# A separate queue for the weight differences of a Strassen-Winograd MLP behind lightning attention, with a new order of loads

## The chip, the cores and the metric

The kernel runs on one core of one Trainium2 chip. The metric is device time in microseconds (us), the median of three runs. Five engines matter: TensorE (PE) multiplies matrices, VectorE (DVE), ScalarE (ACT) and GpSimd (POOL) work elementwise, and the queue of SyncE (SP) starts every load and store. Each engine works off its own instruction stream in order: an instruction that waits holds up all that stands behind it on that engine.

## The reference

```python
# q, k, v: (4, 8, 768, 64), lam: (8,), w_in: (512, 2048), w_out: (2048, 512), all float32; block = 64
for b in range(nb):
    intra = np.einsum('bhic,bhjc->bhij', qb, kb) * Dmask[None]
    intra = np.einsum('bhij,bhjd->bhid', intra, vb)
    inter = np.einsum('bhid,bhde->bhie', qb * lam_pow[None], kv_state)
    out[:, :, sl] = intra + inter
    kv_state = lam_block * kv_state + np.einsum('bhsd,bhse->bhde', kb * rev_pow[None], vb)
x = out.transpose(0, 2, 1, 3).reshape(3072, 512)
h = x @ w_in
g = np.maximum(0.01 * h, h)
return g @ w_out
```

Lightning attention runs in blocks of 64 tokens, with a state per head that is carried from block to block. Its result, 3,072 tokens of 512 values, goes through a two-layer MLP with a leaky ReLU. The weights reach the chip as 64-bit numbers (512 KB for 128 x 512 of them), and the kernel turns them into float32 itself.

## The kernel before

**Attention.** The tokens come in 24 chunks of 128 (six for each batch element). `load` (L328) fetches one chunk: k and q in two pieces each, v in one, 768 KB in all. A chunk passes through a step of three parts (`step`, L481): the products and sums of the chunk before (`own`, `inter`), the transposes of k and q (`transpose_k`, `transpose_q`), and the scores with the update of the state (`scores`, `kv`, `sums_kv`). The copies of the transposes are on ACT, the masking of the scores (`sc`, L403), the update of the state (L430) and, at first, the scaling of q (`qsT`, L388) on DVE, the decay of k (L379) and of the state (L433) on POOL.

**The MLP.** Four chunks make a group (six groups, g), and the hidden dimension is cut into four units (u). For each (g, u) there is an `up` (L568) and a `down` (L600). Each is one step of Strassen-Winograd: seven products P1 to P7 of half-size blocks instead of eight, each of eight 128 x 128 x 256 matmuls. There are 48 stages of `up` or `down` (6 x 4 x 2), so 336 products. The products come in the order P1, P2, P6, P5, P7, P3, P4. P1 and P2 need only blocks of the weights as they are; P6, P5 and P4 need the *differences* of weight blocks T2, T1 and T4 (L318), and P6, P5, P7 and P3 need sums of the left operand (`xs` for `up`, `gS` for `down`, L555). Two PSUM banks, Z and W, alternate; a product waits until the bank was copied or added off (`keep` on ACT or DVE, `total` on DVE).

**The weights.** They come in 32 blocks of 128 hidden columns (n = 0 to 31): for unit u, four blocks of w_in (wi), then four of w_out (wo). Blocks n and n+1 (n even) make a pair, pair n // 2. `load_w` (L217) fetches a block, `conversion` (L244) queues what makes float32 of it: on ACT `magnitude`, `low_part`, `sign_part` (L270, L281, L284); for a pair on DVE `clamp`, `shift`, `first`, `low` (L289, L293, L298 twice); then three subtractions T1, T2, T4 (L305), on DVE for the pairs in `T_DVE`, on POOL for the others.

**The order of the work.** The instruction streams are written by a planner that runs when the kernel is built. It keeps a clock for each engine (`clk`) and an estimated time at which each result is ready. `run` (L176) emits one piece of work. Before that it fills the wait: the conversions lie in the lists `later["ACT"]`, `later["DVE"]`, `later["POOL"]`, first in, first out, and `emit` takes the head of the engine's list when by the estimate it ends no later than the awaited input plus `SLACK`. The slack is 0.55 us while `alone` is true, that is, while attention runs with no MLP beside it, and zero after that. `need(n)` (L199) emits everything that belongs to blocks below n, whatever the clocks say, and then issues every load that has room. `pump` (L209) issues loads in the order of the string `LOADS` ("c" a chunk, "w" a weight block), passing over those that have no room yet (a chunk c needs chunk c-3 finished), as long as the clock of the loads is less than `AHEAD` in front of the PE's.

The kernel begins with nine parts (three steps) of attention alone, then `need(4)`, the rest of what chunk 2 and the front of what chunk 3 needs, P1 and P2 of the first `up` with the scores and state of chunk 3 between, `early(3)`, the sums of the first group (`x_sums(0)`), and `FIRST` parts of the next step (L668 to L679). After that, each `up` or `down` takes along as many parts of attention as `STEPS` says for it (L680 to L684):

```python
    for n, (g, u, w) in enumerate((g, u, w) for g in range(NG) for u in range(NU) for w in range(2)):
        need((2 * u + w + 1) * NW // (2 * NU))
        together((up, down)[w](g, u) if n else parts, STEPS[n] if n < len(STEPS) else 3 * (w == 0))
```

Of the kernel before, what the change touches and what calls it, by code (L numbers as in the profile page):

```python
# [59 lines left out]
def kernel(  # L60
# [20 lines left out]
    NCH = B * NCB  # L81
    GC = 4
    NG = NCH // GC
    T = GC * C // 2
# [72 lines left out]
    ROOMS = ["st"] + [f"{w}{p}" for w, p, h in reversed(blocks) if h == 0 and p >= UP]  # L157


    LOADS = "cwwcwwcwccwwwcwwwccccwcwwwwwwwwwwwwwwwwwwww" + "c" * NCH  # L160
    SLACK, AHEAD = (0.55, 0), (8.0, 14.0)

    T_DVE = [0, 1, 3, 7, 9, 11, 14]

    FIRST, STEPS = 2, [3, 2, 1, 5, 4, 6, 3, 4, 0, 0, 1, 2, 0, 0, 0, 4]
    rooms = {}
    w_raw, lo, w_done = {}, {}, 0

# [2 lines left out]


    clk = {"PE": 0.0, "ACT": 2.0, "DVE": 8.0, "POOL": 1.0, "DMA": 0.5}
    ready, later = {}, {"ACT": [], "DVE": [], "POOL": []}

    def run(eng, us, fn, after=(), gives=None, fill=True):  # L176
        t = max([ready.get(k, 0.0) for k in after], default=0.0)
        if fill and eng in later:
            while later[eng] and emit(eng, t + SLACK[alone]):
                pass  # L180
        clk[eng] = max(clk[eng], t) + us
        fn()
        if gives is not None:
            ready[gives] = clk[eng] + 0.1
        if eng != "DMA":
            pump()

    def emit(eng, until):

        can, us, fn, after, gives = later[eng][0]  # L190
        if not can() or any(k not in ready for k in after):
            return False
        if max([clk[eng]] + [ready[k] for k in after]) + us > until:
            return False
        later[eng].pop(0)
        run(eng, us, fn, after, gives, fill=False)
        return True

    def need(n):  # L199

        while any(later[e] and later[e][0][4][1] < n for e in later):
            m = sum(map(len, [*later.values(), *loads.values()]))
            for e in later:
                while later[e] and later[e][0][4][1] < n and emit(e, 1e9):
                    pass
            pump(urgent=True)
            assert sum(map(len, [*later.values(), *loads.values()])) < m

    def pump(urgent=False):  # L209
        while urgent or clk["DMA"] < clk["PE"] + AHEAD[fin > 3]:  # L210
            able = [x for x in sorted(y[0] for y in loads.values() if y) if x[2]()]
            if not able:
                return
            loads[able[0][1]].pop(0)
            able[0][3]()

    def load_w(n):  # L217
        w, p, h = blocks[n]
        f = p + NP * h
        rooms[n] = room_free(n)  # L220
        pool, size = (tp, 2 * d_model) if rooms[n] == "st" else (wop, 7 * QB)
        t = pool.tile([P, size], F32, name="ws", tag=rooms[n], bufs=1)
        w_raw[n] = t[:, 0:2 * d_model].bitcast(I64)

        def go():
            if w == "wi":
                nc.sync.dma_start(out=w_raw[n].rearrange("p (ko f) -> p ko f", ko=KO), in_=w_in_r[:, :, f * P:(f + 1) * P])
            else:
                nc.sync.dma_start(out=w_raw[n], in_=moe_w_out[f * P:(f + 1) * P, :])

        run("DMA", 1.95, go, [("lowp", m) for m in range(n) if rooms[m] == rooms[n]], ("raw", n))
        ready["raw", n] += 2.0
# [5 lines left out]
    def taken():  # L238
        return {rooms[m] for m in w_raw}
# [4 lines left out]
    def conversion(n, first):  # L244

        kind, p, h = blocks[n]
        W, s = (WI, SI) if kind == "wi" else (WO, SO)

        def dest():
            return W[p][:, 0:4:3, :] if (kind == "wi") == (h == 0) else W[p][:, 1:3, :]

        def words(i, dt):
            return w_raw[n].bitcast(dt).rearrange("p (n two) -> p n two", two=2)[:, :, i].rearrange("p (a b) -> p a b", a=2)

        def may():
            return h == 1 or n <= w_done + 2 and f"{kind}{p}" not in taken()

        def magnitude():
            if h == 0:
                W[p] = wop.tile([P, 7, QB], F32, name=f"{kind}{p}", tag=f"{kind}{p}")
            nc.scalar.activation(out=dest(), in_=words(1, F32), func=AF.Abs)  # L270

        def addend(dt, i):
            t = lo[n].rearrange("p (a b) -> p a b", a=2).bitcast(dt)
            return t.rearrange("p a (b two) -> p a b two", two=2)[:, :, :, i]

        def low_part():
            if h == 0:
                lo[n] = W[p][:, 4:6, :].rearrange("p a b -> p (a b)").bitcast(I32)
            else:
                lo[n] = tp.tile([P, d_model], I32, name="lo", tag="lo", bufs=1)  # L280
            nc.scalar.activation(out=addend(U16, 0), in_=words(0, U32), func=AF.Copy, bias=0.0, scale=2.0 ** -29)  # L281

        def sign_part():
            nc.scalar.activation(out=addend(BF16, 1), in_=words(1, F32), func=AF.Sign, bias=tiny[:, 0:1])  # L284
            del w_raw[n]

        def clamp():
            d = W[p][:, 0:4, :].rearrange("p a b -> p (a b)")
            nc.vector.tensor_scalar(d, d, HI_MIN, HI_MAX, op0=ALU.max, op1=ALU.min)  # L289

        def shift():
            d = W[p][:, 0:4, :].rearrange("p a b -> p (a b)").bitcast(I32)
            nc.vector.tensor_scalar(d, d, 3, None, op0=ALU.logical_shift_left)  # L293

        def low():
            nonlocal w_done
            d = dest().bitcast(I32)
            nc.vector.tensor_tensor(d, d, lo.pop(n).rearrange("p (a b) -> p a b", a=2), op=ALU.add)  # L298
            w_done = n + 1

        def yes():
            return True

        def part(out, a, b, m):
            return lambda: e.tensor_tensor(*(W[p][:, s[i]:s[i] + m, :] for i in (out, a, b)), op=ALU.subtract)  # L305

        later["ACT"].append((may, 0.67, magnitude, [("raw", n)], ("mag", n)))
        later["ACT"].append((lambda: h == 0 or n < w_done + 2, 0.78, low_part, [("raw", n)], ("lo", n)))
        later["ACT"].append((yes, 0.87, sign_part, [("raw", n)], ("lowp", n)))
        if h == 0:  # L310
            return low
        later["DVE"].append((yes, 0.95, clamp, [("mag", n)], ("c", n - 1)))
        later["DVE"].append((yes, 0.95, shift, [], ("s", n - 1)))
        later["DVE"].append((yes, 0.84, first, [("lowp", n - 1)], ("w", n - 1)))
        later["DVE"].append((yes, 0.84, low, [("lowp", n)], ("w", n)))
        eng, e = ("DVE", nc.vector) if n // 2 in T_DVE else ("POOL", nc.gpsimd)

        for o, x, y, m in (("T1", "B12", "B11", 2), ("T2", "B22", "T1", 1), ("T4", "B21", "T2", 1)):  # L318
            us = {"DVE": 0.15 + 0.27 * m, "POOL": 0.13 + 0.75 * m}[eng]
            later[eng].append((yes, us, part(o, x, y, m), [("w", n)], (o, n)))  # L320

    loads = {"c": [], "w": []}

# [4 lines left out]
    def load(c):  # L328
        b, s0 = c // NCB, (c % NCB) * C
        t = []  # L330
        for src, nm, bufs in ((k, "k", 3), (q, "q", 2), (v, "v", 3)):
            x = ldp.tile([P, H, D], F32, name=nm, tag=nm, bufs=bufs)
            y = src[b, :, s0:s0 + C, :]

            def go():
                if nm == "v":
                    nc.sync.dma_start(out=x, in_=y.rearrange("h p d -> p h d"))
                else:
                    for i in range(2):
                        nc.sync.dma_start(out=x[:, i * HP:(i + 1) * HP, :], in_=y[i::2].rearrange("h p d -> p h d"))  # L340

            run("DMA", 1.35, go, [("fin", c - 3)], (nm, c))
            ready[nm, c] += 2.0
            t.append(x)
        loaded[c] = t
# [290 lines left out]
                       lambda name: [PROD[name][0], ("sum", "DVE", PROD[name][0])], u > 0)  # L636


    todo, alone = [], True

    def together(parts, n):

# [13 lines left out]
    for n in range(NW):  # L656
        first = conversion(n, first)
    for i, x in enumerate(LOADS):
        n = len(loads[x])
# [7 lines left out]

    together([], 3 * GC - 3)  # L668
    need(NW // (2 * NU))
    parts, (own_2, whole_3, quads_3) = up(0, 0), step()  # L670
    own_2()
    whole_3()
    alone = False
    parts.pop(0)()
    quads_3()
    parts.pop(0)()
# [38 lines left out]
```

## Time and profile before

| | |
|---|---|
| median of three runs | 701.74 us (700.93 to 703.64) |
| span of the profiled execution | 702.0 us |
| PE busy | 677.3 us (96%) |
| DVE, ACT, POOL busy | 333.4, 217.5, 144.3 us |
| matmuls of the 336 products (L584, L610) | some 0.38 us each as recorded; a product takes 1.73 us |
| subtractions T1, T2, T4 (L305) | 21 on DVE, 27 on POOL |
| loads | 24 chunks of 768 KB, 32 weight blocks of 512 KB |

The page of a profile gives the busy time of each engine, then the span in 40 slices (17.6 us each) with busy shares in tenths, the granted PE clock and the load on the DMA engines. A table of waits names, for each engine, the instruction that stood and the one that released it. The timeline lists instructions in order of time with the idle time before each in brackets, and the table by stages gives the busy time of each engine in chosen stretches. A load counts as landed here when the last of its sixteen completion records in the trace has come.

### The profile page before, as it was taken

The page shows a single profiled execution, that of the slowest core. Times are in us where ns is not written, and L with a number is a line of the kernel's source. Part 1 is how long each engine was busy: PE and PEld are TensorE (multiplying, and loading weights), DVE is VectorE, ACT ScalarE, POOL GpSimd, SP SyncE. Part 2 cuts the span into 40 slices and gives each one's busy share as a digit, 9 for nine tenths or more (in the row PEclk, how much of TensorE's full clock was granted, in tenths as well). Part 3 has the DMA queues.
Part 4 walks back from the last instruction along what each step waited for, and adds up shares of the span by engine and source line. Part 5 has one row for each costly group of instructions (what it writes and reads, how often), then busy time and mean ns, then how long its engine had stood idle before and what let it go on. Part 6 is the DMA issues. An engine that isn't in the chain of part 4 may idle for free.

```text
span 702.0 us, 13353 instructions
## 1 busy us (share of the span) xinstructions
PE 677.3 (96%) x5834; PEld 582.9 (83%) x5834; DVE 333.4 (47%) x493; ACT 217.5 (31%) x361; POOL 144.3 (21%) x139
## 2 busy tenths in 40 slices
PE   6787999999999999999999999999999999999997
PEld 4566888788888888888888888888888888888886
DVE  4769899966314325314245233352433344234324
ACT  4567866551321211321202223113122112221210
POOL 2435355846001005200105102103100003000000
PEclk8879999999999999999999999999999999999999
DMA  9997176533201003302202211000100000100001
GB/s 224 255 268 216 46 202 175 134 96 75 78 1 31 1 0 92 77 1 46 46 1 47 64 43 31 1 2 1 61 1 0 1 0 16 46 0 1 1 0 61
DMA packets 93146, 42.81 MB, mean 61 GB/s; under 512 B 76704, under 2 KB 91040, under 8 KB 93088
## 3 DMA queue, kind: packets, MB, share of 16 engines
q1 hardware_dynamic: 92944, 41.95, 22.4%
q8 instruction: 46, 0.75, 0.5%
q14 instruction: 12, 0.10, 0.1%
q10 hardware_dynamic: 144, 0.00, 0.0%
HBM read 35.66 MB, written 6.29 MB: 60 GB/s over the span
## 4 chain that ended last, share of the span: by engine, by line
PE 87%; DVE 7%; POOL 1%; ACT 1%; DMA 1%; SPq 1%; issue 1%; DVEq 0%; ACTq 0%
PE Z L584 23%; PE Z L610 21%; PE W L584 18%; PE W L610 16%; PE po L351 3%; PE pt L367 2%; PE ps L351 2%; DVE gS L555 2%; PE pu L351 1%; DVE gA L555 1%; DVE wi L298 1%; POOL xs L555 1%; DMA q<-in_q_dram 1%; DVE wi L305 1%; SPq L340 1%
## 5 line engine op out<-in xcount | busy, mean ns | idle before, releaser
L610 PE MATMUL Z<-wo,gA 128*128 128x256 f32 x576 | 137.7, 382 | 0.5 <-DVE os L528 0.5
L610 PEld LDWEIGHTS Z<-wo,gA 128*128 128x128 f32 x576 | 107.5, 190 | 15.3 <-DVE os L528 0.6
L584 PE MATMUL Z<-xs,wi 128*128 128x256 f32 x384 | 92.8, 385 | 3.0 <-DVE xs L555 3.0
L584 PE MATMUL W<-xs,wi 128*128 128x256 f32 x384 | 92.9, 385 | 0.0
L584 PE MATMUL Z<-x,wi 128*128 128x256 f32 x384 | 91.5, 381 | 0.9 <-DVE gA L534 0.9
L610 PE MATMUL W<-wo,gA 128*128 128x256 f32 x384 | 90.8, 379 | 0.0
L530 ACT COPY gA<-Z 128x512 f32<-128x512 f32 x48 | 28.1, 586 | 196.1 <-PE Z L584 196.1
L584 PEld LDWEIGHTS Z<-xs,wi 128*128 128x128 f32 x384 | 73.7, 193 | 13.5 <-DVE xs L555 3.2
L546 ACT ACTIVATE gA<-gA 128x512 f32<-128x512 f32 x72 | 45.3, 630 | 118.5 <-DVE gA L534 118.5
L584 PEld LDWEIGHTS Z<-x,wi 128*128 128x128 f32 x384 | 72.2, 190 | 10.9 <-DVE gA L534 1.1
L610 PEld LDWEIGHTS W<-wo,gA 128*128 128x128 f32 x384 | 72.8, 190 | 9.9
L584 PEld LDWEIGHTS W<-xs,wi 128*128 128x128 f32 x384 | 72.5, 192 | 10.1
L379 POOL TENSOR_TENSOR k<-k,decay 128x512 f32<-128x512 f32 (+1 forms) x24 | 28.1, 1172 | 226.8 <-PE pt L367 221.8
L534 DVE TENSOR_TENSOR gA<-gA,W 128x512 f32<-128x512 f32 x48 | 33.0, 687 | 85.6 <-PE W L584 85.6
L534 DVE TENSOR_TENSOR gA<-gA,Z 128x512 f32<-128x512 f32 x24 | 16.5, 687 | 98.8 <-PE Z L584 98.8
L610 PE MATMUL Z<-wo,gS 128*128 128x256 f32 x192 | 46.0, 382 | 2.7 <-POOL qsT L388 2.2
L610 PE MATMUL W<-wo,gS 128*128 128x256 f32 x192 | 46.1, 383 | 2.3 <-DVE os L534 2.3
L584 PE MATMUL W<-x,wi 128*128 128x256 f32 x192 | 46.4, 385 | 0.0
L534 DVE TENSOR_TENSOR os<-os,W 128x512 f32<-128x512 f32 x48 | 32.8, 683 | 22.4 <-PE W L610 22.4
L610 PEld LDWEIGHTS W<-wo,gS 128*128 128x128 f32 x192 | 35.8, 189 | 8.9 <-DVE os L534 4.1
L610 PEld LDWEIGHTS Z<-wo,gS 128*128 128x128 f32 x192 | 35.9, 190 | 8.5 <-POOL qsT L388 2.6
L433 POOL TENSOR_TENSOR state<-state,pow_q 128x256 f32<-128x256 f32 x40 | 28.4, 709 | 69.0 <-DVE state L430 62.2
(79 smaller groups left out, 741.1 us busy)
## 6 DMA issues: line engine op xcount, KB each, us to landing
ws<-in_moe_w_in_dram SPq DMA_DIRECT2D x16, 512.0 KB, 5.8
ws<-in_moe_w_out_dram SPq DMA_DIRECT2D x16, 512.0 KB, 5.3
k<-in_k_dram SPq DMA_DIRECT2D x48, 128.0 KB, 3.8
q<-in_q_dram SPq DMA_DIRECT2D x48, 128.0 KB, 3.0
v<-in_v_dram SPq DMA_DIRECT2D x24, 256.0 KB, 4.2
out_dram<-os SPq DMA_DIRECT2D x23, 256.0 KB, 2.5
out_dram<-os SPq DMA_DIRECT2D x2, 128.0 KB, 1.8
lam_b<-in_lam_dram ACTq DMA_DIRECT2D x1, 4.0 KB, 2.7
```

Source lines behind the costliest of these rows:

```text
L298: nc.vector.tensor_tensor(d, d, lo.pop(n).rearrange("p (a b) -> p a b", a=2), op=ALU.add)
L305: return lambda: e.tensor_tensor(*(W[p][:, s[i]:s[i] + m, :] for i in (out, a, b)), op=ALU.subtract)
L351: nc.tensor.matmul(out[HALF[cols]], lhsT=lhsT[HALF[rows]], rhs=rhs[HALF[rows]], start=start, stop=True, skip_group_check=True)
L367: nc.tensor.transpose(out=pt[:, y, :], in_=loaded[c][i][:, 2 * y:2 * y + 2, :].rearrange("p a d -> p (a d)"), identity=ident)
L379: run("POOL", 1.2, lambda: nc.gpsimd.tensor_tensor(kr[n], kr[n], _bc(pow_k, 3, D)[n], op=ALU.mult), [("pt", "k")], ("kd", c))
L433: run("POOL", 0.8, lambda: nc.gpsimd.tensor_tensor(state[(m + 1) % 4], new, _bc(lam_c, 2, D), op=ALU.mult), [("state", m)], ("lstate", m + 1))
L530: run("ACT", 0.6, lambda: nc.scalar.copy(dst(i), st[tag]), [tag], f"keep{i}")
L534: lambda: nc.vector.tensor_tensor(dst(i), dst(i), st[tag], op=ALU.add), [f"keep{i}", tag], f"tot{i}")
L546: run("ACT", 0.64, lambda: nc.scalar.activation(out=dst, in_=src, func=AF.Prelu, bias=0.0, scale=1.0, alpha=0.01), [after], gives)
L555: run(eng, us, lambda: e.tensor_tensor(t[o], t[a], t[b], op=op), after, ("sum", eng, o))
L584: nc.tensor.matmul(t[:, i, :], lhsT=w[:, kk, :], rhs=x[:, kk, :], start=(first and i == 0 and kk == 0), stop=(i == UP - 1 and kk == 1), sk ...
L610: nc.tensor.matmul(t[:, m, :], lhsT=G[g, u][sa][:, i, m * P:(m + 1) * P], rhs=WO[UP * u + i][:, SO[sb], :], start=(first and m == 0 and i ...
```

## The change

Three things change, none of which alters what is computed.

The differences T1, T2 and T4 leave the lists of the conversions and get lists of their own, "DVE T" and "POOL T". A list of this kind is looked at after the engine's plain list, and as long as the new flag `held` is true nothing is taken from it, by `run` or by `need`. `held` falls together with `alone`, just ahead of the first product. So while attention runs alone, DVE gets no differences in between, and later they yield to the conversions of the following blocks until `need` calls for them.

The loads come in another order: chunks 1 and 2 each come one weight block after the chunk before instead of two, so that four chunks and four blocks lead instead of four chunks and five blocks, and chunk 4 comes after weight blocks 4 to 7.

The numbers of the plan follow: `SLACK` and `AHEAD` are larger, the pairs whose differences run on DVE are others (pair 1 goes to POOL; 13 and 15 go to DVE), and the parts of attention are spread otherwise over the first sixteen stages (35 parts as before).

```diff
-    LOADS = "cwwcwwcwccwwwcwwwccccwcwwwwwwwwwwwwwwwwwwww" + "c" * NCH
-    SLACK, AHEAD = (0.55, 0), (8.0, 14.0)
-    T_DVE = [0, 1, 3, 7, 9, 11, 14]
-    FIRST, STEPS = 2, [3, 2, 1, 5, 4, 6, 3, 4, 0, 0, 1, 2, 0, 0, 0, 4]
+    LOADS = "cwcwcwwcwwwwcwwwcccwcwwcwwwwwwwwwwwwwwwwww" + "c" * NCH
+    SLACK, AHEAD = (0.7, 0), (10.0, 16.0)
+    T_DVE = [0, 3, 7, 9, 11, 13, 14, 15]
+    FIRST, STEPS = 2, [2, 2, 1, 5, 5, 6, 3, 3, 0, 0, 0, 3, 0, 1, 0, 4]
...
-    ready, later = {}, {"ACT": [], "DVE": [], "POOL": []}
+    ready, later = {}, {"ACT": [], "DVE": [], "DVE T": [], "POOL T": []}
...
-        if fill and eng in later:
-            while later[eng] and emit(eng, t + SLACK[alone]):
+        for e in (eng, eng + " T") if fill else ():
+            while later.get(e) and emit(e, t + SLACK[alone]):
                 pass
...
-        can, us, fn, after, gives = later[eng][0]
-        if not can() or any(k not in ready for k in after):
+        can, us, fn, after, gives = later[queue][0]
+        eng = queue.split()[0]
+        if not can() or held and eng != queue or any(k not in ready for k in after):
             return False
...
-        while any(later[e] and later[e][0][4][1] < n for e in later):
+        queues = [e for e in later if not (held and " " in e)]
+        while any(later[e] and later[e][0][4][1] < n for e in queues):
...
-            later[eng].append((yes, us, part(o, x, y, m), [("w", n)], (o, n)))
+            later[eng + " T"].append((yes, us, part(o, x, y, m), [("w", n)], (o, n)))
...
-    todo, alone = [], True
+    todo, alone, held = [], True, True
...
-    alone = False
+    alone = held = False
```

More of the change, by code (lines that the diff above doesn't have):

```diff
@@ L186, in run, with emit @@
             pump()
-    def emit(eng, until):
-        can, us, fn, after, gives = later[eng][0]
-        if not can() or any(k not in ready for k in after):
+    def emit(queue, until):
+        can, us, fn, after, gives = later[queue][0]
+        eng = queue.split()[0]
+        if not can() or held and eng != queue or any(k not in ready for k in after):
             return False
@@ L194, in emit @@
             return False
-        later[eng].pop(0)
+        later[queue].pop(0)
         run(eng, us, fn, after, gives, fill=False)
@@ L199, in need @@
     def need(n):
-        while any(later[e] and later[e][0][4][1] < n for e in later):
+        queues = [e for e in later if not (held and " " in e)]
+        while any(later[e] and later[e][0][4][1] < n for e in queues):
             m = sum(map(len, [*later.values(), *loads.values()]))
-            for e in later:
+            for e in queues:
                 while later[e] and later[e][0][4][1] < n and emit(e, 1e9):
```

## The prediction

> **What bounds the kernel now.** I read the page's slices first, then the PE's waits, then the timeline of the first 65 us. The slices (17.6 us each):
>
> ```profile
> PE   6787999999999999999999999999999999999997
> DVE  4769899966314325314245233352433344234324
> ...
> PEclk8879999999999999999999999999999999999999
> DMA  9997176533201003302202211000100000100001
> ```
>
> After slice 4 the PE is full to the end; before it, it has holes and a reduced clock, just where the DMA engines are at 9. The stage table says what is left to win:
>
> ```profile
> 26.40:180.00 153.60, 142.31 (x1844) 119.84 (x1843) 122.35 (x166) 90.37 (x148) 79.09 (x71) 0.97 0.59 163
> 180.00:690.00 510.00, 508.98 (x3563) 442.71 (x3562) 190.21 (x282) 111.63 (x190) 56.16 (x52) 1.00 0.08 21
> ```
>
> The columns are stage, length, PE, weight load, DVE, ACT, POOL, clock, DMA share and GB/s. From the first product (26.4) to 180 us the PE stands 153.6 - 142.3 = 11.3 us; from 180 to 690 us only 1.0 us. The products are the same 336 afterwards, so this edit can only win or lose in the first 180 us. The PE's waits:
>
> ```profile
> PE Z L584 <- DVE xs L555: 3.0, 1, 3.0
> PE po L351 <- DVE sc L403: 2.4, 3, 1.2
> PE W L610 <- DVE os L534: 2.3, 3, 1.7
> ...
> PE Z L610 <- POOL qsT L388: 2.2, 1, 2.2
> ...
> PE pu L351 <- DVE qsT L388: 1.7, 1, 1.7
> ```
>
> Nearly all end on DVE. Its timeline, then the PE's, around the first product:
>
> ```profile
> 19.95 2.65 DVE L305 TENSOR_TENSOR wi<-wi 128x512 f32<-128x512 f32 x3
> ...
> 23.12 0.69 DVE L388 TENSOR_TENSOR qsT<-pt,pow_q 128x512 f32<-128x512 f32 x1
> ...
> 27.93 2.35 DVE L305 TENSOR_TENSOR wi<-wi 128x512 f32<-128x512 f32 x3
> 30.20 0.68 DVE L388 TENSOR_TENSOR qsT<-pt,pow_q 128x512 f32<-128x512 f32 x1
> ```
>
> ```profile
> 30.94 0.69 PE L351 MATMUL pu<-v,k 64*64 64x64 f32 x30 [1.67 <-DVE qsT L388]
> 31.56 2.94 PE L584 MATMUL W<-x,wi 128*128 128x256 f32 x8
> ...
> 40.24 3.78 PE L584 MATMUL Z<-xs,wi 128*128 128x256 f32 x8 [2.99 <-DVE xs L555]
> ```
>
> The differences of pairs 0 and 1 (2.65 and 2.35 us) stand directly ahead of attention's work on DVE; the second set makes kv(3), and P2 behind it, wait 1.67 us. P6, the first product that needs any difference, comes only at 40.24, and at half clock (3.78 us instead of 1.93).
>
> **What the skill says.** "SBUF — State Buffer", Who interferes with whom: a DVE instruction with two SBUF inputs blocks against a GpSimd instruction that reads SBUF. The trace agrees: the four sums `xs` take 1.29, 1.65, 0.68 and 0.68 us, the slow two beside POOL's k and qsT. "TensorE: Matmul & The Clock Gate", Part 1, gives half clock after an idle window of about 3.4 us and full clock after a busy one. The trace agrees: clock 0.50 in 40.24 to 44.02, after 2.99 idle us. "GPSIMD Engine Reference", 4.1, calls two-input elementwise work about twice as slow there; here a 128x512 difference is at most 1.7 us on POOL against 0.7 undisturbed on DVE.
>
> **Part by part.**
>
> *Loads.* Landings before: c0 7.05, w0 9.3, w1 10.9, c1 14.4 (its q 13.4), w2 16.1, w3 17.7, c2 22.5, w4 23.9, c3 27.15 (q 26.1), c4 31.4, w5 to w7 32.7, 34.1, 35.5. A block thus takes 1.4 to 1.6 us, a chunk 3.9 to 4.3, its q about 1.1 ahead of its v. In the new order: c1's q 11.8, c2's q some 17.1, w3 some 21.5 (4 later), c3's q 24.6 (1.5 earlier), w4 to w7 27 to 31.2 (w7 4.3 earlier), c4's q some 34.3 (4 later). The sets are equal again after w7 and c4, so the loads behind cost nothing: the same bytes have been moved by then.
>
> *P1.* Steps 1 and 2 start 1.6 and 2.4 us earlier (q landing 13.4 to 11.8, 19.5 or later to 17.1) and no longer wait behind 2.65 us of differences, so they end by about 21.5. Then two arrivals bind. Pair 1 from w3 at 21.5: `magnitude` 0.66, then clamp, shift and first, 3 x 0.7, gives 24.8 with hand-overs. The transposes of q3 at 24.6 plus 0.5 give 25.1. P1 starts at 25.1 instead of 26.4: -1.3.
>
> *P1 to P6.* Before, 13.85 us. The wait for qsT falls (-1.67), because after `low` of pair 1 (25.4) qsT comes at once, at 26.1, and kv(3) at 27.8 finds it done. The sums `xs` may lose up to 1.6 us of blocking or keep it, as POOL now also makes pair 1's T1 and T2 (1.7 + 0.7 to 1.2 us) in this stretch. The half clock: I expect 25.6 to 29.1 cold (PE about half busy before it), costing 1.7, against 0.98 + 0.70 = 1.7 before (clock 0.66 in 2.87 us and 0.75 in 2.82): no change. So xs S2 is done at 25.1 + 13.85 - 1.67 - (0 to 1.6) = 35.7 to 37.3, and P6 is not before 34.8 in any case, since the transposes of c4 (q4 34.3) stand ahead of it on the PE. I take 36.0: **-4.2** against 40.24. The differences of pair 0 cost DVE 1.4 (undisturbed) to 2.65 us; the DVE idle times after 31.5 (0.73, 1.29, 1.39 us) show gaps while P2 and the inter products run, so I cost them at nothing. Bound: if they fall behind the sums, +1.1 to 2.65 plus S3 and S4 (1.36).
>
> *P6 and P5 at half clock.* Before: 0.50 x 3.78 + 0.37 x 2.82 = 2.9 us lost, two windows. With a shorter wait, one window, 1.6 lost: **-1.3**. Bounds 0 and -2.9.
>
> *The waits at 57 to 65 us.* P6 and P5 of the first `down` stand 2.23 and 1.74 us. The first is not POOL's qsT but the copy of os on ACT (60.24 to 60.82), behind conversions; the second is the sum of os on DVE, behind four conversions. Pair 1's 2.35 us leave DVE, and w5 to w7 land 3 to 4 us earlier, into DVE's idle 4.09 us at 43.4. But everything must also be done 5.5 us earlier: from 31.5 to about 48.6 DVE has 14.5 to 18.7 us of work in 17.1. I take 3.97 down to 2.5: **-1.5**, bounds -3.97 and +2.
>
> *75 to 180 us.* PE idle now about 2.8 us (0.13, 0.67, 1.38, 0.49 in 20 us stages, and less). DVE, 60 to 140 us, is busy 73 of 80. Six us less for the same work must cost something; pairs 13 and 15 add some 3.5 us to it, though after 120, where it has room (13.5 of 20). The parts of attention are 35 as before, moved by one stage. I take **+1.0**, bounds 0 and +4.
>
> The sum is -4.2 - 1.3 - 1.5 + 1.0 = -6.0: 701.7 - 6.0 = 695.7 us.
>
> **The rivals.** *DVE takes it back* (a wait in the place of the one removed). Start -4.2, clock -1.3, waits at 57 to 65 as they were and 2 us more ahead of the first `down`, +1.2 later: -2.3, 699.4. For it: DVE at 73 of 80 and 14.5 to 18.7 us in 17.1. Against it: 19 idle us of DVE before 60. *All the early waits vanish*: -4.2 - 2.9 - 4.0 = -11.1, 690.6. For it: 11.3 idle and 4.6 cold us lie there. Against it: loads still fill the DMA engines to 57 us. *Starved differences*, slower: their list comes second, so with DVE 90% busy they wait until `need` calls them just ahead of the stage, and P6 two products later finds them unfinished, above all POOL's sets of 3 to 4 us. First stage 3 late, some 7 later stages by 1 each, 57 to 65 worse by 3: -4.2 + 3 + 7 + 3 = +8.8, 710.5. Against it: two products and attention parts are 3.5 us or more, and POOL is busy only 79 of 153.6 us.
>
> **The numbers.** Likeliest -6.0 (0.58), DVE takes it back (0.22), all waits vanish (0.12), starved (0.08). Range 689.5 to 701.5: the lower end takes in -11.1, the upper the -2.3 with a bound term missed by 2; it leaves out the starved case and the tails. Faster (under 698.2) is nearly all of the first and third, 0.70; same 0.20; slower (over 705.2) 0.10.
>
> **What would show it.** Right: no L305 on DVE before the first product; P1 at 24 to 26 us; no wait of pu for qsT; P6 at 35 to 37; waits in the first `down` under 4 us; PE idle after 75 us under 4. Wrong: P6 waiting for L305 or for q of chunk 4 beyond 37; P1 later than 26.4 because w3 lands later; new PE waits on DVE between 75 and 180 us of more than 4 us.

## The result, and the profile after

The changed kernel takes 693.07 us (median of four runs, 691.17 to 695.40); the kernel before, run beside it, 701.72 us. The ratio is 0.9874 (95% interval 0.9835 to 0.9914): faster by 8.65 us, where 6.0 were forecast. The profiled spans lie further apart, 702.0 against 689.4 us, because the profiled execution of before was one of its slowest (703.8 us) and that of after its fastest (691.17 us). So the medians say how much was won, and the profiles where.

The slices of the page after, in the same four rows as shown of before:

```profile
PE   7789999999999999999999999999999999999997
DVE  5797899982342543324426324344333244224324
...
PEclk9999999999999999999999999999999999999999
DMA  9999545623001004220210301000100000100001
```

The PE is full from the fourth slice on instead of the fifth, and the reduced clock in slices 1 to 3 is gone. The stage table (columns as before: stage, length, PE, weight load, DVE, ACT, POOL, clock, DMA share, GB/s):

```profile
25.30:180.00 154.70, 151.76 (x1837) 128.79 (x1836) 124.05 (x177) 94.65 (x156) 72.78 (x64) 0.99 0.59 161
180.00:677.00 497.00, 495.98 (x3568) 431.12 (x3567) 185.91 (x276) 107.61 (x184) 57.38 (x54) 1.00 0.08 22
```

From the first product to 180 us the PE now stands 2.9 us instead of 11.3; behind 180 us it is 1.0 us as before. Of the waits that are left on the PE:

```profile
...
PE Z L587 <- DVE xs L558: 2.0, 1, 2.0
PE pt L370 <- DMA q<-in_q_dram: 1.9, 4, 1.3
...
PE Z L613 <- DVE os L531: 0.7, 2, 0.5
PE W L613 <- DVE os L537: 0.5, 2, 0.3
```

The wait for qsT is gone, and those of the first `down` too. The third and fourth product (P6 and P5) of the first `down`, before and after:

```profile
60.92 1.97 PE L610 MATMUL Z<-wo,gS 128*128 128x256 f32 x8 [2.23 <-POOL qsT L388]
64.63 1.99 PE L610 MATMUL W<-wo,gS 128*128 128x256 f32 x8 [1.74 <-DVE os L534]
```

```profile
51.16 1.89 PE L613 MATMUL Z<-wo,gS 128*128 128x256 f32 x8
52.89 1.89 PE L613 MATMUL W<-wo,gS 128*128 128x256 f32 x8
```

DVE and PE around the first product (lines are 3 higher in the changed file):

```profile
26.17 0.68 DVE L391 TENSOR_TENSOR qsT<-pt,pow_q 128x512 f32<-128x512 f32 x1
26.77 1.37 DVE L308 TENSOR_TENSOR wi<-wi 128x512 f32<-128x512 f32 x1
```

```profile
25.06 0.44 PE L370 MATMUL pt<-ident,q 128*128 128x128 f32 x2 [1.30 <-DMA q<-in_q_dram]
25.34 3.42 PE L587 MATMUL Z<-x,wi 128*128 128x256 f32 x8
...
29.54 0.64 PE L354 MATMUL pu<-v,k 64*64 64x64 f32 x32
...
36.60 1.99 PE L587 MATMUL Z<-xs,wi 128*128 128x256 f32 x8 [1.97 <-DVE xs L558]
38.43 1.89 PE L587 MATMUL W<-xs,wi 128*128 128x256 f32 x8
```

qsT now stands ahead of the first difference, P1 waits for q of chunk 3, and P6 and P5 run at full clock, while P1 is the cold one, that is, the one at half clock (3.42 us). Four marks show where the time went (start of each on the PE, from the timelines, us):

| kernel | P1 of the first up | its P6 | P1 of the first down | P1 of the next up | span | ratio to before |
|---|---|---|---|---|---|---|
| before | 26.39 | 40.24 | 55.08 | 74.11 | 702.0 | 1 |
| after | 25.34 | 36.60 | 47.60 | 62.09 | 689.4 | 0.9874 |
| e1 hold only | 26.19 | 37.15 | 50.76 | 69.18 | 713.2 | 1.0172 |
| e2 loads only | 24.48 | 38.17 | 50.13 | 68.84 | 696.8 | 0.998 |
| e3 after, old loads | 27.57 | 39.55 | 52.76 | 67.23 | 694.7 | 0.9895 |
| e4 after, no hold | 25.13 | 41.13 | 53.66 | 68.14 | 695.6 | 0.9915 |
| e5 after, old T_DVE | 24.88 | 36.68 | 49.28 | 63.76 | 694.9 | 0.9913 |
| e6 after, old STEPS | 26.18 | 37.96 | 51.40 | 71.98 | 699.3 | 0.9967 |
| e7 after, old SLACK | 25.56 | 35.73 | 47.07 | 61.57 | 691.2 | 0.9859 |
| e8 before, new STEPS | 27.96 | 38.81 | 51.27 | 67.27 | 704.6 | 1.0057 |
| e9 before, PE kept busy | 26.52 | 38.85 | 50.80 | 69.82 | 697.7 | 0.998 |
| e10 after, PE kept busy | 25.78 | 36.37 | 48.82 | 63.30 | 690.6 | 0.9853 |
| e11 after, STEPS 3, 1 | 24.94 | 36.66 | 48.62 | 68.80 | 697.7 | 0.9959 |
| e12 before, STEPS and T_DVE | 27.57 | 39.81 | 52.48 | 66.95 | 703.3 | 1.0048 |

Each row is one execution, and executions of one instruction stream differ. Up to P5 of the first `up`, after, e6 and e11 have the same streams: their P1 starts at 25.34, 26.18 and 24.94, their P6 at 36.60, 37.96 and 36.66. Before and e8 have the same streams up to there too: P1 at 26.39 and 27.96, P6 at 40.24 and 38.81. So a mark that moves by less than some 1.5 us shows nothing by itself, and P6 comes earlier by something between 0.9 and 3.6 us.

From the last mark to the end, before takes 702.0 - 74.1 = 627.9 us and after 627.3. All that was won lies ahead of it: 12.0 us in these two profiles, of which 1.05 up to P1, 2.6 from P1 to P6, 3.8 from P6 to the first `down`, and 4.5 in the first `down`. (0.86 us of it is one part of attention that comes later now.)

### The profile page after: what moved, and what is told of

Read it like the earlier page. It is cut to its first block, busy times and chain, and to the rows that moved or that the text cites. A ratio compares the mean times of both kernels' runs of the same rounds, so it can differ in the third digit from the quotient of the medians.

```text
span 689.4 us, 13357 instructions
## 1 busy us (share of the span) xinstructions
PE 672.5 (98%) x5834; PEld 578.5 (84%) x5834; DVE 330.2 (48%) x496; ACT 216.7 (31%) x361; POOL 140.4 (20%) x136
## 4 chain that ended last, share of the span: by engine, by line
PE 89%; DVE 5%; SPq 2%; DMA 2%; POOL 1%; issue 1%; ACT 1%; DVEq 0%
PE Z L587 24%; PE Z L613 22%; PE W L587 18%; PE W L613 17%; PE po L354 3%; PE pt L370 2%; PE ps L354 2%; DMA q<-in_q_dram 2%; DVE gS L558 1%; PE pu L354 1%; SPq L343 1%; DVE gA L558 1%; POOL wo L308 1%; DVE os L537 0%; SPq L230 0%
## 5 line engine op out<-in xcount | busy, mean ns | idle before, releaser
L587 PE MATMUL Z<-xs,wi 128*128 128x256 f32 x384 | 90.9, 380 | 2.0 <-DVE xs L558 2.0
L613 PEld LDWEIGHTS W<-wo,gA 128*128 128x128 f32 x384 | 72.6, 190 | 10.0
L537 DVE TENSOR_TENSOR os<-os,W 128x512 f32<-128x512 f32 x48 | 32.8, 683 | 24.6 <-PE W L613 24.6
```

The source lines that it names most:

```text
L537: lambda: nc.vector.tensor_tensor(dst(i), dst(i), st[tag], op=ALU.add), [f"keep{i}", tag], f"tot{i}")
L587: nc.tensor.matmul(t[:, i, :], lhsT=w[:, kk, :], rhs=x[:, kk, :], start=(first and i == 0 and kk == 0), stop=(i == UP - 1 and kk == 1), sk ...
L613: nc.tensor.matmul(t[:, m, :], lhsT=G[g, u][sa][:, i, m * P:(m + 1) * P], rhs=WO[UP * u + i][:, SO[sb], :], start=(first and m == 0 and i ...
```

## The experiments

The prediction's theory, A: the differences on DVE and the order of loads together set the chain to P6, and what they free removes the waits behind it. B: the order of loads alone. C: the new numbers of the plan (`STEPS`, `T_DVE`). Each change of a number is a change of the whole plan, so the four marks were read as well as the time.

### One part alone, one part undone (e1 to e4)

**e1**, the lists and the hold alone, that is, the changed kernel with all four lines of numbers as before:

```diff
-    LOADS = "cwcwcwwcwwwwcwwwcccwcwwcwwwwwwwwwwwwwwwwww" + "c" * NCH
-    SLACK, AHEAD = (0.7, 0), (10.0, 16.0)
-    T_DVE = [0, 3, 7, 9, 11, 13, 14, 15]
-    FIRST, STEPS = 2, [2, 2, 1, 5, 5, 6, 3, 3, 0, 0, 0, 3, 0, 1, 0, 4]
+    LOADS = "cwwcwwcwccwwwcwwwccccwcwwwwwwwwwwwwwwwwwwww" + "c" * NCH
+    SLACK, AHEAD = (0.55, 0), (8.0, 14.0)
+    T_DVE = [0, 1, 3, 7, 9, 11, 14]
+    FIRST, STEPS = 2, [3, 2, 1, 5, 4, 6, 3, 4, 0, 0, 1, 2, 0, 0, 0, 4]
```

> The kernel before with only the separate lists and the hold; loads, slack, T_DVE and STEPS as before. Theory A (the chain to P6 was set by differences on DVE and by the loads together): no L308 on DVE before the first product, the 1.67 us wait of pu for qsT gone, P1 near 26.6 (bound by q of chunk 3, landing 26.1), P6 near 37.5 to 38.5 instead of 40.24, time about 699. Theory B (the order of loads alone did it): P6 stays near 40, 701.5. Theory C (the new T_DVE and STEPS did it, in the first down): 701.5, and the two waits of the first down stay near 4 us together.

Measured: 715.0 us, ratio 1.0172 (1.0155 to 1.019), slower than before by 12 us. The early part did what A said: P1 26.19, P6 37.15 instead of 40.24, and the next `up` starts at 69.18 instead of 74.11. But then 16 us are lost, most of it at one place, by a wait and by the half clock behind it (163.40 to 173.64 us, with 5.7 us of PE work in it). The PE's timeline, the DVE's and the ACT's of this kernel:

```profile
167.95 2.93 PE L613 MATMUL Z<-wo,gA 128*128 128x256 f32 x6 [8.69 <-DVE wo L301]
```

```profile
161.14 1.75 DVE L292 TENSOR_SCALAR wo<-wo 128x1024 f32<-128x1024 f32 x1
162.93 1.64 DVE L296 TENSOR_SCALAR wo<-wo 128x1024 int32<-128x1024 int32 x1
164.60 1.63 DVE L301 CUSTOM_DVE_ANT_0 wo<-wo 128x1024 uint16<-128x1024 uint16 x1
166.15 1.74 DVE L301 CUSTOM_DVE_ANT_0 wo<-wo,lo 128x1024 uint16<-128x1024 uint16 x1
```

```profile
152.24 0.87 ACT L287 ACTIVATE wo<-ws,tiny 128x512 bf16<-128x512 f32 x1
```

The last `down` of the first group waits for the conversion of the last weight pair. By `room_free` blocks 30 and 31 can only use the one room "st", a staging buffer, so the load of block 31 waits until ACT has read block 30 (152.24 + 0.87 = 153.1). It is issued at 153.1, lands at 157, and its conversion comes to DVE just when POOL makes the sums of the next group (L558, 160.63 to 167.4): the four instructions take 6.8 us instead of some 2.8. None of A, B and C had foreseen this.

**e2**, the new loads alone:

```diff
-    LOADS = "cwwcwwcwccwwwcwwwccccwcwwwwwwwwwwwwwwwwwwww" + "c" * NCH
+    LOADS = "cwcwcwwcwwwwcwwwcccwcwwcwwwwwwwwwwwwwwwwww" + "c" * NCH
```

> The kernel before with only the new string LOADS. Theory A: the steps start 2 us earlier but the differences still stand ahead of qsT, P6 at 38 to 39.5, time 698 to 700. Theory B: P6 near 36.6, time 693 to 695. Theory C: 701.

Measured: 700.72 us, 0.998 (0.9967 to 0.9994), P6 at 38.17, as A expected. The differences of pair 0 stand ahead of the conversion of pair 1 on DVE, and now P1 runs into them:

```profile
23.57 2.65 DVE L305 TENSOR_TENSOR wi<-wi 128x512 f32<-128x512 f32 x3
```

```profile
24.48 1.03 PE L584 MATMUL Z<-x,wi 128*128 128x256 f32 x4
28.43 1.10 PE L584 MATMUL Z<-x,wi 128*128 128x256 f32 x4 [2.92 <-DVE wi L298]
```

The waits of the first `down` stay (1.64 and 2.01 us). B, which had P6 near 36.6 and 693 to 695 us, falls.

**e3**, the changed kernel with the old string `LOADS` (the diff of e2 the other way round):

> The changed kernel with the old string LOADS. Theory A: P1 near 26.6, P6 near 38, time 695 to 697. Theory B: all of it is lost, 700 to 702. Theory C: 693 to 694.

Measured: 695.69 us, 0.9895 (0.9876 to 0.9914; the interval overlaps that of the changed kernel). P1 27.57 and P6 39.55, 1.0 and 1.6 us later than A expected, hardly more than a mark varies; the time is in A's range. But P6 is hardly earlier than before, and still some 7 us are won. The first `down` takes 14.5 us with no wait, though the last of its weights, w7, lands as in before (35.2 and 35.5). So its waits did not hang on the loads.

**e4**, the hold alone undone:

```diff
-    todo, alone, held = [], True, True
+    todo, alone, held = [], True, False
```

> The changed kernel with held false from the start: the lists are separate, but the differences of pair 0 (DVE) and pair 1 (POOL) may be made while attention runs alone. Theory A: pair 0's differences delay sc and qsT of chunks 2 and 3, P6 1 to 2.5 us later (37.5 to 39), time 694 to 696. Theories B and C: no change, 693.

Measured: 697.21 us, 0.9915 (0.9889 to 0.9942; this interval and that of the changed kernel overlap). P6 at 41.13, later by 4.5 us, more than A expected, and not by the way A gave. POOL and ACT of e4:

```profile
27.16 2.88 POOL L308 TENSOR_TENSOR wi<-wi 128x512 f32<-128x512 f32 x3 [4.51 <-DVE wi L301]
30.00 1.06 POOL L382 TENSOR_TENSOR k<-k,decay 128x512 f32<-128x512 f32 x1
```

```profile
36.53 0.63 ACT L273 ACTIVATE wo<-ws 128x512 f32<-128x512 f32 x1
37.07 0.61 ACT L549 ACTIVATE gA<-gA 128x512 f32<-128x512 f32 x1
37.59 0.57 ACT L478 ACTIVATE x<-po 128x512 f32<-128x512 f32 x1
```

Pair 1's differences are on POOL now. Put in early they wait there for `low` and stand ahead of the decay of k, which runs at 30.00 instead of 23.31; kv(3) and P2 follow it (31.74 instead of 30.11). Then the copy of chunk 3's x on ACT stands behind more conversions, at 37.59 instead of 33.47, and P6 waits 5.29 us for the sums of x. So the hold keeps POOL free for attention, and not DVE alone.

### Which number removes the waits of the first down (e5 to e8, e11)

The first `down` takes 14.5 us in after, e3 and e4, and 18.4 to 19.0 in before, e1 and e2. T says: the differences of pair 1, which left DVE. S says: the parts of attention beside the stages.

**e5** and **e6**, the changed kernel with the old `T_DVE` or the old `STEPS`:

```diff
-    T_DVE = [0, 3, 7, 9, 11, 13, 14, 15]
+    T_DVE = [0, 1, 3, 7, 9, 11, 14]
```

> The changed kernel with the old T_DVE (pair 1's differences back on DVE, 13 and 15 on POOL). In the runs so far the stretch from the first down's P1 to the next up's P1 takes 14.5 us with the new plan numbers, whatever the loads and the hold, and 18.4 to 19.1 us with the old ones. Theory T (DVE's load of differences made those waits): the stretch returns to 18 us, time 697. Theory S (the parts of attention laid beside the stages made them): 14.5 us, time 693 to 694. Late in the first group the old places could also delay the last weight blocks.

```diff
-    FIRST, STEPS = 2, [2, 2, 1, 5, 5, 6, 3, 3, 0, 0, 0, 3, 0, 1, 0, 4]
+    FIRST, STEPS = 2, [3, 2, 1, 5, 4, 6, 3, 4, 0, 0, 1, 2, 0, 0, 0, 4]
```

> The changed kernel with the old STEPS (3 parts beside the first up, so the transposes of chunk 5 stand ahead of the first down). Theory S: the stretch from the first down's P1 to the next up's P1 returns to 18 us, time 697. Theory T: 14.5 us, time 693 to 694.

Measured: e5 695.98 us, 0.9913 (0.9893 to 0.9934, which overlaps the changed kernel's), and its first `down` still takes 63.76 - 49.28 = 14.5 us. T falls. Of the 5.5 us by which the profile of e5 is longer than that of after, 1.7 are lost by the next `up`. Most of the rest comes at 139 us, where differences of pair 13, now on POOL again, are late and the products behind them run at half clock:

```profile
139.40 2.07 PE L587 MATMUL Z<-xs,wi 128*128 128x256 f32 x4 [2.08 <-POOL wi L308]
```

e6: 699.68 us, 0.9967 (0.9955 to 0.9978), and its first `down` takes 20.6 us, with waits of 1.03 and 2.89 us. S stands; in time it costs more than S had said.

**e7**, the old `SLACK` and `AHEAD` in the changed kernel:

```diff
-    SLACK, AHEAD = (0.7, 0), (10.0, 16.0)
+    SLACK, AHEAD = (0.55, 0), (8.0, 14.0)
```

> The changed kernel with the old SLACK and AHEAD. Theories S and T both: no part of the gain, 692 to 695. If the slack of 0.7 (how far conversions may push attention back) or the deeper lead of the loads matters, 696 or more.

Measured: 692.53 us, 0.9859 (0.9844 to 0.9874). These two numbers bring nothing that can be told from zero. (In the code `SLACK[alone]` takes the second number, 0, while attention runs alone, and the first, 0.55 or 0.7, from the first product on. The description of the planner above has it the other way round. So the slack acts where the products run, the first `down` among them.)

**e11** moves one part of attention, the transposes of chunk 5, from the first `down` back to the end of the first `up` (the two other parts beside that `up` move by one product with it):

```diff
-    FIRST, STEPS = 2, [2, 2, 1, 5, 5, 6, 3, 3, 0, 0, 0, 3, 0, 1, 0, 4]
+    FIRST, STEPS = 2, [3, 1, 1, 5, 5, 6, 3, 3, 0, 0, 0, 3, 0, 1, 0, 4]
```

> The changed kernel with STEPS beginning 3, 1 instead of 2, 2: the transposes of chunk 5 move from the first down back to the end of the first up, everything else stays. If these transposes, with their two copies on ACT and the work on POOL ahead of the first down, make the waits of the first down: its stretch grows from 14.5 to 17 us or more, time 696 to 698. If not: 693.

Measured: 699.41 us, 0.9959 (0.9939 to 0.9978); the first `down` takes 68.80 - 48.62 = 20.2 us. That is as slow as e6, so this one part makes up all of e6's loss that can be told from zero. PE, ACT and DVE of e11:

```profile
48.18 0.60 PE L370 MATMUL pt<-ident,q 128*128 128x128 f32 x4
48.62 1.89 PE L613 MATMUL Z<-wo,gA 128*128 128x256 f32 x8
50.34 1.89 PE L613 MATMUL W<-wo,gA 128*128 128x256 f32 x8
53.62 1.96 PE L613 MATMUL Z<-wo,gS 128*128 128x256 f32 x8 [1.38 <-issue]
58.69 2.54 PE L613 MATMUL W<-wo,gS 128*128 128x256 f32 x8 [3.11 <-DVE os L537]
61.02 3.08 PE L613 MATMUL Z<-wo,gA 128*128 128x256 f32 x8
```

```profile
52.46 0.57 ACT L375 COPY qT<-pt 128x512 f32<-128x512 f32 x1
52.93 0.59 ACT L533 COPY os<-Z 128x512 f32<-128x512 f32 x1
```

```profile
53.40 1.75 DVE L558 TENSOR_TENSOR gA<-gA,gS 128x512 f32<-128x512 f32 x1
55.08 0.68 DVE L301 CUSTOM_DVE_ANT_0 wi<-wi,lo 128x1024 uint16<-128x1024 uint16 x1
55.68 0.68 DVE L292 TENSOR_SCALAR wi<-wi 128x1024 f32<-128x1024 f32 x1
56.39 1.65 DVE L296 TENSOR_SCALAR wi<-wi 128x1024 int32<-128x1024 int32 x1
57.96 0.67 DVE L537 TENSOR_TENSOR os<-os,W 128x512 f32<-128x512 f32 x1
```

P1 ends near 50.4 and P2 near 52.2, but ACT copies P1's bank only at 52.93, behind conversions and the copies of kT and qT, and DVE adds P2's bank only at 57.96, behind three conversions of the *next* stage. Why were they put there? The planner's own clocks, printed while it wrote the streams, say: in e11 and in before it believes q of chunk 5 to be ready at 52.85, while its PE clock is at 48.20 (48.17 in before). So it takes the PE to stand for some four us ahead of the first `down` and fills this time on ACT and DVE with conversions. The pattern is that of before, where ACT copies P1's bank at 60.24, behind conversions too. On the chip q of chunk 5 lands at 46.4 in e11 (47.4 in after), its transposes run at 48.18 with no wait, and the filling is in the way: 1.38 + 3.11 = 4.5 us of wait, and half clock on the next products (2.54 and 3.08 us instead of 1.9). Some 2 us of DVE's delay come from two instructions that take 1.75 and 1.65 us, where such ones take 0.69 with POOL idle; POOL's qsT and its differences run beside them. With 2, 2 the transposes come when the planner's clock has passed 55, it expects no wait, and nothing is put in for their sake. That the false estimate does the harm, more than the transposes' own two copies (1.1 us on ACT), is read from these lines and clocks; no run corrected the estimate alone.

**e8**, the new `STEPS` in the kernel before (the diff of e6 the other way round, in that kernel):

> The kernel before with only the new STEPS; no hold, old loads and T_DVE. Theory S: P6 stays near 40, the stretch from the first down's P1 to the next up's P1 falls from 19.1 to 15 us, time 697 to 699. Theory T: no gain, 701 to 703.

Measured: 706.53 us, 1.0057 (1.004 to 1.0075), slower. S was right on the stretch (16.0 us, of which 1.25 a wait for a conversion in P1, and 67.27 instead of 74.11 at the next `up`) and wrong on the end. **e12** adds the new `T_DVE`:

> The kernel before with the new STEPS and the new T_DVE; old loads, no hold. The new STEPS alone won 7 us by 67 us and lost 9 later, 5.35 of it waiting for the last weight pair on DVE and 0.9 for differences on POOL. If the new T_DVE is what mends that: no such waits, time 696 to 698. If the loads or the hold mend it: the waits stay, 702 to 707.

Measured: 705.49 us, 1.0048 (1.0034 to 1.0061). The wait for pair 13's differences is gone, that for the last pair stays in both:

```profile
159.61 2.93 PE L610 MATMUL Z<-wo,gA 128*128 128x256 f32 x6 [5.35 <-DVE wo L298]
```

(this line is of e8; that of e12 has the same 5.35 us at 157.92). The half clock behind this wait (157.10 to 163.93 us in e12, with 6.0 us of PE work in it) costs some 3 us more. Together this is more than the 7 us won. Block 31 lands at 149 us in before and in e12, at 151 in e8. In before its conversion (150.3 to 153.0 on DVE) is done 6 us ahead of the `down` that needs it, at 158.68. With the PE 7 us ahead, the `down` starts at 151.98 (e12), and half of the conversion falls beside POOL's sums. In after block 31 lands at 138, in e3 at 143, in e4 at 144, in e7 at 139, and none of them waits. Each of these three leaves out one thing: the new loads (e3), the hold (e4), the new `SLACK` and `AHEAD` (e7). So none of them is needed by itself to get the last block there in time. e12 has none of the three, and no separate lists either. Which of these four would be enough was not taken apart.

### The half clock (e9, e10)

**e9** keeps the PE busy while it stands for xs in the kernel before:

```diff
     together([], FIRST)
+    hot = pp.tile([P, HP, C], F32, name="hot", tag="pt", bufs=2)
+    for _ in range(18):
+        nc.tensor.transpose(out=hot[:, 0, :], in_=ident, identity=ident)
```

> The kernel before with 18 spare transposes of the identity on the PE between the transposes of chunk 4 and P6, in the time in which the PE stands for xs; nothing else is changed. If the half clock after that stand costs what was worked out (2.9 us on P6 and P5) and the stages behind pass it on: P6 1.9 and P5 1.7 us long instead of 3.8 and 2.8, time 698.5 to 700. If ACT and DVE bind the first down anyway, P6 and P5 are short but the first down's waits grow by as much: 701 to 702.5.

Measured: 700.61 us, 0.998 (0.9968 to 0.9992), 1.4 us less than before.

```profile
36.21 2.18 PE L682 MATMUL hot<-ident 128*128 128x128 f32 x18 [0.36 <-ACT kT L372]
38.85 1.99 PE L584 MATMUL Z<-xs,wi 128*128 128x256 f32 x8 [0.46 <-DVE xs L555]
...
56.64 3.56 PE L610 MATMUL Z<-wo,gS 128*128 128x256 f32 x8 [2.22 <-POOL qsT L388]
```

P6 and P5 are short (1.99, 1.89), and the clock is at half again behind the next stand, at 56.64. The 2.9 us are what P6 and P5 lost in one execution of before; in e8, with the same streams up to there, they lose some 1.5 (3.48 and 1.89 us). So how much of such a gain is passed on stays open. **e10** does the same ahead of P1 in the changed kernel (11 transposes between those of k and of q of chunk 3):

> The changed kernel with 11 spare transposes between the transposes of k and of q of chunk 3, while the PE stands for q of chunk 3. P1 2 us long instead of 3.4, P6 up to 1.4 us earlier if the chain from P1 to xs binds, but no earlier than the transposes of chunk 4 (q of chunk 4 lands near 34.2) allow: 691.5 to 693. No gain would say that the half clock at P1 is hidden behind the landing of chunk 4.

Measured: 692.56 us, 0.9853 (0.9822 to 0.9884), not to be told from the changed kernel. P1 is no longer cold (two pieces of 1.03 and 1.10 us), but P6 is:

```profile
36.37 3.46 PE L587 MATMUL Z<-xs,wi 128*128 128x256 f32 x8 [1.33 <-DVE xs L558]
```

The transposes of chunk 4 end at 35.05 and P6 then waits for xs, so P1's 1.4 us were hidden up to there. That the spare work moved the half clock from P1 to P6 is not shown: in e6, which has the streams of after up to P5 and no spare work, P6 is cold as well:

```profile
37.96 3.47 PE L587 MATMUL Z<-xs,wi 128*128 128x256 f32 x8 [2.36 <-DVE xs L558]
```

No version was found that is clearly faster than the changed kernel.

## Why the prediction was right, point by point

The direction and the bound (only the first 180 us can move) held, and the time lies in the range, 2.6 us under the forecast. But most of the gain came from a part of the change that the prediction had put at nothing. By its steps:

- **Loads.** c1's q 11.3 (forecast 11.8), c2's q 16.9 (17.1), w3 21.6 (21.5), c3's q 25.0 (24.6), w7 32.05 (31.2), c4's q 34.15 (34.3). Right, though the 3.9 to 4.3 us given for a chunk is narrower than the landings of before, where the four chunks behind c0 land 3.2 to 4.9 us after the load ahead of them.
- **P1** at 25.34, forecast 25.1, released by q of chunk 3 as said (24.94 and 26.18 in e11 and e6). Right.
- **P6** at 36.60, forecast 36.0: -3.6 for -4.2 in this pair of profiles, -0.9 to -3.6 over the profiled executions of the two streams, so the forecast was too large. The wait for qsT fell away as said, in after and with the hold alone (e1). The cold window from 25.6 to 29.1 came as forecast (25.53 to 28.95), which is in part luck: in e11 and e6 it runs from 22.45 to 29.28 and from 23.93 to 30.75. e4 adds what the step had not seen: the hold matters through POOL and ACT, 4.5 us at P6.
- **P6 and P5 at half clock.** Forecast -1.3 (one cold window for two), with -2.9 as the bound. In after both run at full clock; in e6, with the same streams up to there, P6 is cold (3.47 us), as the forecast had it. Which of the two comes changes from execution to execution.
- **The waits of the first down.** Forecast -1.5; measured -3.97, no wait is left. The size was in the bounds, but **the step's reason fell**: "Pair 1's 2.35 us leave DVE, and w5 to w7 land 3 to 4 us earlier". With pair 1 back on DVE (e5), or the old loads (e3), there is no wait either; with both as new and the old `STEPS` (e6) the waits are 1.03 and 2.89 us, as long as before. Moving one part of attention (e11) brings back 4.5 us. The prediction had put the parts at nothing by themselves ("35 as before, moved by one stage"). They were the largest single piece: their old values take 0.9874 to 0.9967 (e6), some 6.5 us.
- **75 to 180 us.** Forecast +1.0 of new waits, with room for the new pairs on DVE "after 120". That is misread: the 13.5 busy us of 20 are those from 140 to 160; from 120 to 140 DVE was busy 19.3 us. The waits did not come all the same. From 62 to 182 us the PE stands 0.95 us in after and 4.41 in before, of which 1.74 belongs to the first `down`: about -1.7. DVE, busy 72.6 of the 80 us from 60 to 140 in after, was no bound.
- **The rivals.** "DVE takes it back" did not come in after, but it is what happens to parts of the change: in e8 and e12 the 7 us won by the `STEPS` are given back at the last weight pair. "All the early waits vanish" (-11.1, 690.6) is nearest to the profile; in the medians the result lies between it and the likeliest case. "Starved differences" showed only as 2.08 us in e5, on POOL, as that rival said, and pair 13 on DVE is what avoids it (e12).

Of the parts tried alone, one gives 0.2% (e2) and two make it slower (e1, e8); all together give 1.3%. The hold and the loads bring the start forward, and the `STEPS` take a false expectation out of the plan. That the last weights then come early enough to keep this needs more than `STEPS` and `T_DVE`; what exactly is open.

That the sum came out near was in good part luck. Start and clock were to give 5.5 us. With all of the change but the `STEPS` (e6), 699.68 us stand against 702.15 before: 2.5 us are won in all. The term for the parts of attention was missing, the first `down` was set too low for a reason that fell, and the new waits after 75 us did not come.

## What to carry to other kernels

When a planner with estimated times writes the streams, compare its estimates with the landings in the trace. Here one load believed 5 to 6 us later than it comes put conversions ahead of urgent work on two engines. That cost some 6 us (e11), more than holding back the differences is worth in the same kernel (some 3 us in e4, with overlapping intervals). Work that moves the front forward by some us must be followed to the next thing with fixed timing (here the last weight block, through its single staging room), or it is given back there: e1, e8 and e12 reach the second `up` 5 to 7 us earlier than before and end later. Queue filler work apart from urgent work on every engine on which urgent work follows it, and not only on the busiest. Before reading a mark of a single profile, see how far it moves between executions of one stream; here it was 1.5 us.

## What the runs showed of the hardware that was not expected

Where the half clock falls is not fixed by the instruction streams. After, e6 and e11 have the same streams up to P5 of the first `up`. In after the clock is at half from 25.53 to 28.95, in e11 from 22.45 to 29.28, in e6 from 23.93 to 30.75 and again from 37.58 to 40.99. In before it is so from 11.97 to 18.80, from 32.45 to 35.87 and from 39.28 to 46.11; in e8, with the same streams up to P5, from 21.37 to 28.20 and from 38.44 to 41.85. All these windows last 3.41 us or twice that (10.24 us, three times that, in e1 and e9).

The stand ahead of such a window was shorter than the window here. The prediction cites an idle window as what brings the half clock, and finds P6's stand of 2.99 us to agree with that. The clock records differ: in before the half clock begins at 39.28, inside that stand, and in the 3.41 us ahead of it the PE had 1.4 us of work; ahead of 32.45 it had 1.7, ahead of 25.53 in after 1.8, ahead of 21.37 in e8 2.2. So the PE was not idle for a whole window in any of these. No lowest share of work that keeps the clock full was found.

Spare work may keep the clock full over a stand. In the profile of e9, with eighteen 128 x 128 transposes in 2.18 us ahead of P6, the clock stays full from 19.30 to 56.85, where before and e8 fall to half ahead of P6.
